# Loading v in four-token runs, w_in in halves, and a written-out order for the first seventeen attention slots

## Chip, cores and metric

One core of a Trainium2 chip runs the whole kernel. The metric is device time in microseconds (us) of one execution. Five engines work side by side, each through its own instructions in the order in which they were written: TensorE (PE in the profile: matmuls, and transposes done as matmuls; PEld is its weight load), VectorE (DVE), ScalarE (ACT), GpSimd (POOL) and SyncE (SP), which here only issues DMAs. GpSimd issues those DMAs that change the type on the way (float32 to bfloat16).

## The reference

Eight batches of eight heads, 576 tokens, head size 64: attention over a sliding window of 128 tokens with a bias that falls linearly with distance, and its output (4,608 rows of 512) through a two-layer network with a hard-swish in between.

```python
scores = scale * np.matmul(q, k.transpose(0, 1, 3, 2))
rel = pos[:, None] - pos[None, :]
bias = slopes[:, None, None] * (-np.abs(rel).astype(np.float32))[None, :, :]
mask = (rel >= 0) & (rel < window)            # window = 128
scores = np.where(mask, scores + bias[None], -1000000000.0)
attn = np.exp(scores - np.max(scores, axis=-1, keepdims=True))
attn = attn / (np.sum(attn, axis=-1, keepdims=True) + 1e-09)
attn_out = np.matmul(attn, v)
# x = attn_out as [4608, 512]
h = x @ w_in                                   # w_in [512, 2048]
g = h * np.clip(h + 3.0, 0.0, 6.0) / 6.0
out = g @ w_out                                # w_out [2048, 512]
```

All inputs and the output are float32; the matmuls run in bfloat16.

## The kernel before

**Attention.** Two heads make a pair, so there are 32 pairs ("slots" in the steady part), four to a batch: pairs 0 to 3 are batch 0, pairs 4 to 7 batch 1. For a pair, q and k are wanted with the head size on the partitions. For batch 0 they come as nine-token runs (`load_run`, line 90), are cast by `prepare` (line 204), transposed on TensorE by 18 small matmuls for q and 18 for k (`transposes`, line 211) and copied out of PSUM. For batches 1 and 2, and for half of batch 3, four heads are transposed together, nine full transposes at a time (`prepare_double` line 223, `wide_double` line 248, `double` line 236). The rest goes through `tbuf` and a transposing DMA (`xbar`, line 197). `scores_diag` (line 285) and `scores_off` (line 313) are 8 and 10 matmuls of 64 rows, two heads in turn, for the block on the diagonal and the block beside it; `tables_diag` and `tables_off` (lines 266 and 299) add bias and mask by matmuls for the first pairs. ScalarE takes the exponential, GpSimd masks where no table did. `attend` (line 406) or `values` (line 394) multiply by v with a column of ones and divide by the sum. `back` (line 421) turns the result so that the model dimension lies on the partitions (the ring `xT`): by five transposes on TensorE and a copy for pairs 0 to 7, 10 and 11, by a transposing DMA issued by SP for the others.

**v.** `load_tokens` (line 108) brings v with one token on each partition, which makes the pieces 256 bytes long. `cast_v` (line 179) or `cast_tokens` (line 183) cast it into `vbuf`.

**The network.** Tokens go in nine groups of 512. A unit "up" (`moe_up`, line 462) is four matmuls of 512 columns, ScalarE's part of the activation and VectorE's; sixteen of them fill `gbuf`. A unit "down" (`moe_down`, line 488) is four matmuls of 512 columns; four of them make 128 rows of the output. `load_w_in` brings a quarter of w_in (line 165), `load_w_out` a quarter of w_out (line 170), both on GpSimd's queue. The probabilities of batch 0 are kept in the room of `w_out_sb`, those of batch 1 in `gbuf[1]` (`rooms`, line 274).

**Order.** Nothing is reordered by a compiler: every engine works in the order of the code. `first_batch` (line 558) does the four pairs of batch 0 whole, then `second_batch` (line 618) works batch 1 with up units between, and `segment` (line 669) works slots 8 to 31, each slot with seven or eight units put in by `fill` (line 523), which takes them from the list `units`. After the last slot only units are left.

## Time and profile before

| | |
|---|---|
| median of three runs | 323.52 us (323.32 to 324.7) |
| the profiled execution, its own time | 323.3 us |
| its span, first to last instruction | 321.6 us |
| granted TensorE clock, mean | 0.998 |
| first matmul of an up unit | at 22.0 us |
| first matmul of a down unit | at 51.71 us |
| first matmul of the last rows of the output | at 314.98 us |

The span is divided in the page into 40 slices of some 8 us. A digit is the busy share of an engine in tenths, 9 being 90% or more. "Busy" of a matmul runs to its modelled end, and matmuls overlap, so a stretch can count as busy although the next matmul starts late; the distances between starts in the timeline show that. A row of the timeline names the start, the length, the engine, the line of the kernel, what is written from what, and how many alike were merged; an idle time before it stands in brackets with what ended it.

### The profile page before, as it was taken

The page shows a single profiled execution, that of the slowest core. Times are in us where ns is not written, and L with a number is a line of the kernel's source. Part 1 is how long each engine was busy: PE and PEld are TensorE (multiplying, and loading weights), DVE is VectorE, ACT ScalarE, POOL GpSimd, SP SyncE. Part 2 cuts the span into 40 slices and gives each one's busy share as a digit, 9 for nine tenths or more (in the row PEclk, how much of TensorE's full clock was granted, in tenths as well). Part 3 has the DMA queues.
Part 4 walks back from the last instruction along what each step waited for, and adds up shares of the span by engine and source line. Part 5 has one row for each costly group of instructions (what it writes and reads, how often), then busy time and mean ns, then how long its engine had stood idle before and what let it go on. Part 6 is the DMA issues. An engine that isn't in the chain of part 4 may idle for free.

```text
span 321.6 us, 7050 instructions
## 1 busy us (share of the span) xinstructions
PE 312.4 (97%) x2738; PEld 167.6 (52%) x2738; DVE 173.0 (54%) x338; ACT 195.6 (61%) x334; POOL 141.1 (44%) x249
## 2 busy tenths in 40 slices
PE   7889999999999999999999999999999999999996
PEld 5565465455555554554667654554554444444443
DVE  6667674554456555555555555555655455455510
ACT  3758976877767766766676667666764344244401
POOL 8455493594493767366745665463331000000000
PEclk9999999999999999999999999999999999999999
DMA  7999999899999999999999989922112200000112
GB/s 276 202 333 208 247 270 196 210 258 194 212 248 166 244 201 203 193 229 199 192 199 202 237 173 212 214 72 86 23 53 66 75 34 35 33 33 33 67 53 77
DMA packets 131425, 51.90 MB, mean 161 GB/s; under 512 B 118976, under 2 KB 123328, under 8 KB 131392
## 3 DMA queue, kind: packets, MB, share of 16 engines
q1 hardware_dynamic: 126160, 45.36, 66.2%
q0 software_dynamic: 4224, 4.19, 8.2%
q10 hardware_dynamic: 1008, 1.90, 1.6%
q8 instruction: 21, 0.34, 0.5%
q14 instruction: 12, 0.10, 0.1%
HBM read 36.70 MB, written 9.44 MB: 143 GB/s over the span
## 4 chain that ended last, share of the span: by engine, by line
PE 82%; DMA 10%; SPq 2%; POOL 2%; DVE 1%; ACT 1%; issue 1%; POOLq 0%
PE ops L501 37%; PE hps L451 33%; DMA w_out_sb<-in_moe_w_out_dram 5%; DMA ldbuf<-in_v_dram 3%; PE scd L296 3%; DMA ldbuf<-in_k_dram 2%; PE av L391 2%; SPq L112 2%; PE av L383 2%; PE sco L328 1%; PE ops L482 1%; PE w L153 1%; POOL w_out_sb L171 1%; PE tp L219 0%; ACT kTb L244 0%
## 5 line engine op out<-in xcount | busy, mean ns | idle before, releaser
L471 DVE SCALAR_TENSOR_TENSOR gbuf<-r,hps 128x512 bf16<-128x512 f32 x144 | 98.7, 687 | 102.5 <-ACT r L470 100.2
L470 ACT ACTIVATE r<-hps,bias 128x512 f32<-128x512 f32 x144 | 98.9, 689 | 88.9 <-PE hps L451 88.7
L451 PE MATMUL hps<-xT,w_in_sb 128*128 128x512 bf16 (+1 forms) x640 | 144.8, 358 | 0.5 <-ACT xT L438 0.3
L501 PE MATMUL ops<-w_out_sb,gbuf 128*128 128x512 bf16 x560 | 137.8, 379 | 0.3 <-DMA w_out_sb<-in_moe_w_out_dram 0.3
L451 PEld LDWEIGHTS <-w_in_sb 128*128 128x128 bf16 x640 | 59.2, 98 | 54.8 <-issue 0.8
L501 PEld LDWEIGHTS <-gbuf 128*128 128x128 bf16 x560 | 51.8, 98 | 56.7 <-issue 0.6
L354 POOL TENSOR_SCALAR_AFFINE_SELECT pd<-pd 128x512 bf16<-128x512 bf16 x48 | 29.7, 634 | 34.5 <-ACT pd L351 34.5
L364 POOL TENSOR_SCALAR_AFFINE_SELECT po<-po 128x512 bf16<-128x512 bf16 x48 | 30.3, 636 | 32.5 <-ACT po L361 32.3
L351 ACT ACTIVATE pd<-scd,bias_d 128x512 bf16<-128x512 f32 x48 | 31.7, 685 | 4.7 <-PE scd L296 4.7
L510 DVE COPY osb<-ops 128x512 f32<-128x512 f32 x33 | 22.7, 687 | 20.4 <-PE ops L501 20.2
L361 ACT ACTIVATE po<-sco,bias_o 128x512 bf16<-128x512 f32 x48 | 33.0, 688 | 0.0
L194 POOL CAST tbuf<-ldbuf 128x512 bf16<-128x512 f32 (+1 forms) x45 | 25.6, 614 | 16.7 <-DMA qTb<-tbuf 9.0
L402 DVE TENSOR_TENSOR avs<-av,rc 128x384 bf16<-128x384 f32 (+1 forms) x48 | 23.6, 491 | 1.6
L391 PEld LDWEIGHTS <-pd 128*128 128x128 bf16 x192 | 14.3, 97 | 8.3 <-issue 0.5
L383 PE MATMUL av<-vbuf,po 128*128 128x65 bf16 x192 | 18.0, 193 | 0.0
L391 PE MATMUL av<-vbuf,pd 128*128 128x65 bf16 x192 | 17.3, 194 | 0.3 <-ACT kTb L244 0.3
L187 POOL CAST vbuf<-ldbuf 128x1024 bf16<-128x1024 f32 x14 | 14.3, 1044 | 4.3 <-DMA ldbuf<-in_v_dram 4.3
L383 PEld LDWEIGHTS <-po 128*128 128x128 bf16 x192 | 14.3, 98 | 2.9 <-DVE avs L402 0.5
L367 ACT ACTIVATE p4buf<-sco,bias_d 128x64 bf16<-128x64 f32 x48 | 15.5, 324 | 0.0
L227 POOL CAST pr<-ldbuf 128x576 bf16<-128x576 f32 x20 | 12.9, 670 | 5.0 <-DMA ldbuf<-in_k_dram 3.1
L296 PE MATMUL scd<-qTb,kTb 64*128 64x128 bf16 x256 | 12.7, 219 | 1.7 <-DVE kTb L220 0.9
L296 PEld LDWEIGHTS <-kTb 64*128 64x128 bf16 x256 | 7.2, 94 | 13.4 <-issue 9.7
(96 smaller groups left out, 217.4 us busy)
## 6 DMA issues: line engine op xcount, KB each, us to landing
out_dram<-osb SPq DMA_DIRECT2D x33, 256.0 KB, 2.4
ldbuf<-in_v_dram SPq DMA_DIRECT2D x32, 256.0 KB, 5.6
ldbuf<-in_q_dram SPq DMA_DIRECT2D x20, 256.0 KB, 4.9
ldbuf<-in_k_dram SPq DMA_DIRECT2D x16, 256.0 KB, 4.5
ldbuf<-in_q_dram SPq DMA_DIRECT2D x12, 288.0 KB, 7.3
ldbuf<-in_k_dram SPq DMA_DIRECT2D x12, 288.0 KB, 7.6
w_in_sb<-in_moe_w_in_dram POOLq DMA_DIRECT2D x4, 512.0 KB, 8.8
w_out_sb<-in_moe_w_out_dram POOLq DMA_DIRECT2D x4, 512.0 KB, 11.6
```

The source lines that it names most:

```text
L194: nc.gpsimd.tensor_copy(out=tbuf[:m, :, j, :], in_=s[:m, j, :, :].rearrange("p (i e) d -> p i (e d)", e=2))
L296: nc.tensor.matmul(scd[:, e, ts(j, 128)], lhsT=kT[r, j, :], rhs=qT[r, j, :], start=first, stop=first or j == 3)
L351: nc.scalar.activation(out=pd[:, e, :, :].rearrange("p j c -> p (j c)"), in_=sc[:, e, :], func=ACT.Exp, bias=bias_d[:, h:h + 1], scale=scale)
L354: nc.gpsimd.affine_select(out=pd[:, e, :, :], in_=pd[:, e, :, :], pattern=[[0, 4], [1, 128]], channel_multiplier=-1, base=0, compare_op=AL ...
L361: nc.scalar.activation(out=po[:, e, :, :].rearrange("p j c -> p (j c)"), in_=sc[:, e, :], func=ACT.Exp, bias=bias_o[:, h:h + 1], scale=scale)
L364: nc.gpsimd.affine_select(out=po[:, e, :, :], in_=po[:, e, :, :], pattern=[[0, 4], [-1, 128]], channel_multiplier=1, base=-1, compare_op=A ...
L383: nc.tensor.matmul(out_av, lhsT=po[:, e, qt % 4, :], rhs=vb[:, qt - 1, h, :], start=True, stop=False)
L391: nc.tensor.matmul(out_av, lhsT=d, rhs=vb[:, qt, h, :], start=(qt == 0), stop=True)
L451: nc.tensor.matmul(hps[:, lo:hi], lhsT=w_in_sb[:, ks, ts(ms, 128)], rhs=xT[:, ks, ds(src, hi - lo)], start=(ks == 0), stop=(ks == n_ks - 1))
L470: nc.scalar.activation(out=r6, in_=hps, func=ACT.Relu, bias=bias3[:, 0:1], scale=1.0 / 6.0)
L471: nc.vector.scalar_tensor_tensor(out=gts[nt][:, ms, :], in0=r6, scalar=1.0, in1=hps, op0=ALU.min, op1=ALU.mult)
L501: nc.tensor.matmul(ops[nt, sub], lhsT=gts[nt][:, ms, ts(sub, 128)], rhs=w_out_sb[:, ms, :], start=(ms == 0), stop=(ms == n_ms - 1))
```

## The change

Seven parts, all of them in the part of the kernel before slot 20.

- v of batches 0 and 1 is loaded with four consecutive tokens on a partition (`s_ldv`), two DMAs of four heads each for tokens 0 to 511, in pieces of 1,024 bytes; the last 64 tokens still come token by token (`s_ldl`, cast by `s_cl`). Two casts (`s_cr`) put it into `vruns`, which lies in `tbuf`. Matmuls with a selection matrix put the tokens back in order: `s_vp` makes two groups of 128 tokens, eight matmuls of 32 rows and 512 columns, in two row groups by turns, and `s_ve` copies each group of 128 tokens from PSUM into `vbuf`. The selection matrix `sel` is made on VectorE at the start by one memset and 16 small copies.
- w_in is loaded by two DMAs of half its columns (`s_wp`) in place of four of a quarter (`load_w_in`).
- The results of pairs 4, 5 and 6 go to `xT` by a transposing DMA (`s_bx`); pair 7 still goes by TensorE.
- The products with v of batch 0 are cut differently: `s_vf` makes the first three groups of 128 tokens of a pair, `s_vr` one group of several pairs at once, `s_vl` four groups of pair 3. The backs of batch 0 are four groups a pair, and one matmul group for the last 64 tokens of all four pairs (`s_br`).
- `warm_up` issues 27 matmuls in place of 30; `p4buf` has four buffers in place of two.
- `first_batch`, `second_batch` and the slots up to 19 are replaced by `PLAN`, a text with one step a line, which `run_plan` issues in order; an argument V, P or A names the engine of a copy. Each engine gets its own steps out of it in the order of the lines. `segment` starts at slot 20. The order of up and down units between (`ORDER`) is fitted to it.
- In the plan the loads and the masks of slots 8 to 16 stand in another order, too: loads of the next batches are spread piece by piece among the other steps.

The steps named below: `c0` casts and `t0` transposes q or k of a pair of batch 0, `e0` copies the result; `td`, `to`, `sd`, `so` are the tables and scores; `xt`, `xd`, `xo` exponentials; `pd`, `dt`, `de` cast, transpose and copy four heads of a later batch; `vf`, `vr`, `vl` multiply by v, `nf`, `nr`, `nl` divide; `bf` transposes back and `ef` copies to `xT`; `u` is the four matmuls of an up unit, `ur` and `um` its activation. After the part of the plan that is printed come the other fifteen up units of the first group of tokens, the second batch with `vp 1 0 h o` and `vp 1 2 h av`, the four `wout`, which stand between the up units, `bx 5`, `bx 4`, `bx 6`, `bk 7`, and then `d 0 0 0 h`, the first down unit, behind five up units of the second group.

```diff
+    sel = perm.tile([128, 4 * 130], BF16)
...
-    def second_w_in():
-        nc.gpsimd.memset(w_out_sb[:, 4, 0:1], 0.0)
-        load_w_in(1)
...
-    ORDER = [("UUDUDUUDUD", "UUDUDUDUD", "UDUDUDD", "UUDDDD"),
+    ORDER = [("UUDUDUUDUDUUDUDUDUDUDUDUDDUUDDDD",),
...
-    def first_batch():
-        prepare(0, (V, A))
...
-    def second_batch():
-        for g in range(NP, 2 * NP - 1):
...
+    def s_c0(g, nm, eng):
+        pr = prs.tile([128, RT * D], BF16, tag=f"pr{nm}", name="pr",
+                      padded_shape=[128, 2 * RT * D])
+        C[eng](out=pr, in_=runs[nm][:, g % NP, :])
+        st[g, nm] = pr
...
+    def quads(tag, n):
+        if tag == "sc":
+            return psum(tag, 1024).rearrange("p (g c) -> p g c", c=256)[:, 0:n, 0:2 * W].rearrange(
+                "p g (e c) -> p g e c", e=2)
+        return psum(tag, n * 2 * W).rearrange("p (g e c) -> p g e c", g=n, e=2)
...
+    def s_vf(g, tag):
+        av = st["vf", g] = quads(tag, 3)
+        av_matmuls(g, range(3), lambda qt, e: av[:, qt, e, :])
...
+    def s_vr(g0, n, qt, tag):
+        av = st["vr", g0, qt] = quads(tag, n)
+        for i in range(n):
+            av_matmuls(g0 + i, (qt,), lambda _, e: av[:, i, e, :])
...
+    def s_ub(nt, ms, n, tag):
+        hps = psum(tag, 512)
+        up_mms(nt, ms, 0, n, hps)
+        st["u", nt, ms] = hps, n
...
+    def s_u(nt, ms, tag):
+        hps, n = st.get(("u", nt, ms), (None, 0))
+        if hps is None:
+            hps = psum(tag, 512)
+        up_mms(nt, ms, n, n_ks, hps)
+        st["u", nt, ms] = hps, n_ks
+        at[0] += 1
...
+    SEL = sel[:, 0:4 * 129].rearrange("p (t c) -> p t c", t=4)
+    vruns = tbuf.rearrange("p h j c -> p (h j c)")[:, 0:4 * H * D].rearrange(
+        "p (t h d) -> p t h d", t=4, h=H)
+
+    def s_sel():
+        nc.vector.memset(sel, 0.0)
+        diag = sel.rearrange("p (t c) -> p t c", t=4)[:, :, 0:128:4]
+        for j in range(4):
+            r = slice(32 * j, 32 * j + 32)
+            for t in range(4):
+                nc.vector.tensor_copy(out=diag[r, t, :], in_=ident[r, r])
...
+    def s_ldv(b, h, n):
+        nc.sync.dma_start(out=vsource(b)[0][:, ds(h, n), :],
+                          in_=v[b, ds(h, n), 0:512, :].rearrange("h (p t) d -> p h (t d)", t=4))
...
+    def s_cr(b, h, n, eng):
+        C[eng](out=vruns[:, :, ds(h, n), :].rearrange("p t h d -> p h t d"),
+               in_=vsource(b)[0][:, ds(h, n), :].rearrange("p h (t d) -> p h t d", t=4))
+
+    def unshuffle(b, h, n, j0, banks):
+        for t in range(4):
+            for i, ps in enumerate(banks):
+                r = slice(32 * (j0 + i), 32 * (j0 + i) + 32)
+                nc.tensor.matmul(ps, lhsT=SEL[r, t, 0:128], rhs=vruns[r, t, ds(h, n), :],
+                                 start=(t == 0), stop=(t == 3))
...
+    def s_vp(b, j0, t1, t2):
+        banks = [psum(t, 512).rearrange("p (h d) -> p h d", h=H) for t in (t1, t2)]
+        for i in range(2):
+            st["vu", b, 0, j0 + i] = banks[i].rearrange("p (j h) d -> p j h d", j=1)
+        unshuffle(b, 0, H, j0, banks)
+
+    def s_ve(b, h, n, j0, nj, eng):
+        C[eng](out=vbuf[b % 2][:, ds(j0, nj), ds(h, n), 0:D], in_=st["vu", b, h, j0])
+
+    def s_wp(i, k0, n):
+        nc.gpsimd.dma_start(out=w_in_sb[:, ds(k0, n), ts(i, 1024)],
+                            in_=moe_w_in[ds(k0 * 128, n * 128), ts(i, 1024)].rearrange(
+                                "(k p) f -> p k f", p=128))
...
+    def s_bx(g):
+        b, hp = divmod(g, NP)
+        nc.sync.dma_start_transpose(
+            out=xT[:, hp, ds(b % 4 * S, SP)].rearrange("p (j c) -> p j c", j=NQ),
+            in_=st[g, "avs"].rearrange("p j e d -> p (j e d)"))
...
+    def run_plan(text):
+        for line in text.split("\n"):
+            if line.strip():
+                name, *args = line.split()
+                STEPS[name](*(int(a) if a.isdigit() else a for a in args))
...
+    PLAN = """
+sel
+wu 20
+td 0
+wu 7
+c0 0 k A
+c0 0 q A
+mem 3
+t0 0 k o
+e0 0 k V
+ldv 0 4 4
+c0 1 q A
+c0 2 k P
+t0 0 q h
+e0 0 q A
+ldv 0 0 4
+t0 1 q o
+c0 1 k A
+sd 0
+xt 0
+to 0
+t0 1 k h
+e0 1 k A
+c0 2 q P
+t0 2 k h
+ldd 1 0 q 1
+c0 3 q V
+ldl 0
+e0 1 q V
+cr 0 4 4 V
+cr 0 0 4 P
+td 1
+e0 2 k A
+so 0
+t0 3 q h
+ldd 1 0 q 0
+xo 0
+c0 3 k V
+ldd 1 1 k 1
+sd 1
+t0 2 q o
+xt 1
+to 1
+ldd 1 0 k 0
+so 1
+td 2
+e0 2 q V
+sd 2
+xo 1
+ldd 1 0 k 1
+t0 3 k h
+e0 3 k V
+to 2
+xt 2
+e0 3 q V
+vp 0 2 o av
+so 2
+xo 2
+vp 0 0 h h
+ve 0 0 8 3 1 V
+ve 0 0 8 0 1 A
+ve 0 0 8 2 1 V
+ve 0 0 8 1 1 V
+vf 0 av
+td 3
+pd 1 0 k 0 V
+pd 1 0 k 1 V
+to 3
+vr 0 3 3 o
+ldd 1 1 k 0
+wp 0 0 4
+vf 2 h
+mem 2
+pd 1 0 q 0 P
+nr 0 3 3
+nf 2
+sd 3
+so 3
+xt 3
+pd 1 0 q 1 P
+vf 1 o
+nf 1
+xo 3
+nf 0
+dt 1 0 q 0 9 sc
+cl 0 P
+bf 1 h
+ef 1 0 512 A
+mem 4
+de 1 0 q 0 9 V
+bf 0 h
+vl 3
+pd 1 1 k 0 P
+bf 2 h
+pd 1 1 k 1 P
+vr 2 2 4 av
+nl 3
+dt 1 0 k 0 9 sc
+ldv 1 4 4
+de 1 0 k 0 9 V
+cr 1 4 4 P
+nr 2 2 4
+ef 0 0 512 A
+bf 3 o
+to 5
+ldd 1 1 q 0
+ef 3 0 256 A
+vr 0 2 4 h
+wp 1 0 4
+ef 2 0 512 A
+ldd 1 1 q 1
+sd 5
+ef 3 256 256 A
+xd 5 1
+pd 1 1 q 0 V
+so 5
+u 0 5 h
...
             load_run(g, "q", nc.sync)
-        load_tokens(0, "v")
         constants()
         memsets()
-        memsets_later()
-        first_batch()
-        second_batch()
-        fill(2)
-        segment(2 * NP, G, lambda g: FILLS.get(g, (1, 1, 1, 2, 0, 1, 2)))
+        run_plan(PLAN)
+        done[0] = 20 - 1
+        segment(20, G, lambda g: FILLS.get(g, (1, 1, 1, 2, 0, 1, 2)))
         done[0] = G
         fill(len(units))
 
```

## The prediction

> **What bounds the kernel now.** I read the page's engine shares first, then the sums by stage, then TensorE's timeline of the stages that are not full, then the DMAs that these stages wait for.

> ```profile
> span 321.6 us, 7050 instructions
> PE 312.4 (97%) x2738; PEld 167.6 (52%) x2738; DVE 173.0 (54%) x338; ACT 195.6 (61%) x334; POOL 141.1 (44%) x249
> ...
> PE   7889999999999999999999999999999999999996
> ```

> ```profile
> 0.00:8.00 8.00, 5.83 (x74) 4.64 (x76) 4.80 (x31) 2.80 (x4) 6.49 (x21) 1.00 0.78 275
> 8.00:16.00 8.00, 6.96 (x178) 4.28 (x180) 4.92 (x9) 6.00 (x6) 3.36 (x5) 1.00 1.09 204
> 16.00:24.00 8.00, 6.64 (x127) 5.39 (x128) 5.44 (x12) 4.37 (x7) 4.76 (x8) 1.00 1.10 333
> 24.00:52.00 28.00, 27.50 (x315) 15.74 (x313) 18.97 (x30) 24.42 (x37) 18.73 (x29) 1.00 1.14 235
> 52.00:96.00 44.00, 43.03 (x374) 22.24 (x373) 22.39 (x43) 31.71 (x58) 27.30 (x46) 1.00 1.08 222
> 96.00:240.00 144.00, 144.00 (x1280) 78.49 (x1279) 80.83 (x161) 97.30 (x181) 78.97 (x139) 1.00 0.92 174
> ```

> After the stretch come busy times of TensorE, its weight load, VectorE, ScalarE, GpSimd, then clock, DMA share and GB/s. From 96 us TensorE is full, and ScalarE, the next, has 97.30 of 144 us. So the change can win only before 96 us, and every matmul that it adds costs its full time unless it falls into a wait. The idle sum before 96 us is 6.0 us (96 less 89.97), and the timeline shows waits that the sum hides:

> ```profile
> 43.71 0.59 PE L451 MATMUL hps<-xT,w_in_sb 128*128 128x512 bf16 x2
> 44.44 0.45 PE L432 MATMUL tb<-ident,avs 128*128 128x128 bf16 x5
> ...
> 46.14 0.44 PE L432 MATMUL tb<-ident,avs 128*128 128x128 bf16 x5
> 46.73 0.45 PE L242 MATMUL tp<-ident,pr 128*128 128x128 bf16 x5
> ...
> 47.61 0.45 PE L432 MATMUL tb<-ident,avs 128*128 128x128 bf16 x5
> 48.27 0.38 PE L242 MATMUL tp<-ident,pr 128*128 128x128 bf16 x4 [0.21 <-ACT kTb L244]
> ...
> 57.70 1.03 PE L451 MATMUL hps<-xT,w_in_sb 128*128 128x512 bf16 x4
> 59.05 1.02 PE L501 MATMUL ops<-w_out_sb,gbuf 128*128 128x512 bf16 x4 [0.33 <-DMA w_out_sb<-in_moe_w_out_dram]
> ```

> Four matmuls of 512 columns take 0.86 us where nothing waits (the chain shows them so throughout), a transpose of 128 columns 0.056. So 57.70 to 59.05 hides 1.35 - 0.86 = 0.49 us of waiting for w_out; the three rows before it hide 0.30, 0.31 and 0.38 us beside the turning back of pairs 4 to 6. In the same way I find 0.30 at 54.8, 0.33 and 0.15 at 71 to 73, 0.14 and 0.34 at 79 to 81, and 0.18, 0.23 and 0.24 from 89 to 92: together 3.4 us of waits between 25 and 96 us.

> **The change, part by part.**

> *The selection matmuls.* The trace has no 32-row matmul. The nearest rows are the scores: 64 rows, two heads in turn, eight of 128 columns from start to next work in 0.33 us, where eight full ones take 0.45; starts lie 3 and 28 ns apart by turns, so two row groups run together. If the 32-row ones do the same, eight of 512 columns take four times 0.216 = 0.87 us, else 1.73. I take 0.87, since the form is the same but for the rows, and keep 1.73 for the range. [...] Here a change to the scores and back costs 0.10 and 0.12 us over the plain distance, so I add 0.2: 1.07 us a `vp`, 4.3 us for four. The two of batch 0 are in the chain below; the two of batch 1 stand among up units, where TensorE is full: **+2.1 us**.

> *Their copies.* Each group of 128 tokens is one PSUM copy of 512 columns, 0.69 us on VectorE by the `osb` row (0.59 on ScalarE). Four a batch replace the five casts of v (0.56 each on VectorE, 0.62 on GpSimd), and the two casts of runs (1.04 us by the 1,024-element GpSimd row) come on top. In batch 1 the up units cover them (VectorE 18.97 of 28 us); without that cover a copy would hold `av` for 0.7 us. The selection matrix is 17 small VectorE operations, some 0.07 each by the bias rows (eight in 0.58): 1.2 us, under ScalarE's casts, which end later.

> *The first 25 us, by hand.* TensorE finishes 27 warm-ups and one set of tables at 5.14 (in place of 30 and two sets at 6.45). The first k cast ends at 5.4 as before, q's now follows on ScalarE; its copy ends at 7.15, so the first scores start at 7.2 (before: 7.94). ScalarE's copies and VectorE's cast of q of pair 3, whose load lands near 9, hold the second scores to 10.15 (10.26). VectorE then takes the first half of v. Runs end near 9 and v passes 4,096 packets of 256 bytes now; half of it as 512 long ones lands near 11, so that cast ends at 12 and the third scores start at 12.95 (13.12). GpSimd's half lands near 12.3 and ends at 13.6. `vp 0 2` runs to 15.1, `vp 0 0` to 16.25. Here is the first new wait: `vf 0` needs all four copies, the last at 17.1: 0.85 us in which `td 3`, `to 3` and pair 3's scores queue behind it, with their exponentials. From there the exponentials of pair 3 (two of 0.95 us) and VectorE's divisions (0.6 each) and copies (1.35) give `dt` at 20.4, `vl` at 21.4, `dt 1 0 k` at 22.25, `sd 5` at 24.35 and the first up unit at 25.0. Before, the first up matmul runs at 22.0, and by 25.0 seven are done (1.5 us), transposes for 0.75 and the row back of 0.22; after, transposes for 1.0 and the tables and scores of pair 5 for 1.2 are done ahead. That is 2.5 against 2.2 us of work, within my rounding: **0.0 us**. So 1.07 us a `vp` and the new wait are paid with the earlier start and fuller slots, not saved.

> *Pairs 4 to 6 by DMA.* Fifteen transposes go: 15 x 0.056 = **-0.84 us**, and 3 ScalarE copies of 0.64 us. The transposing DMAs have 22 rows in the trace, 2.5 us to landing; the tokens are wanted by the second group of up units, more than 4 us later. SP must wait for the divided result, and behind it stand the next loads of q and v; the trace has SP's loads waiting 2 us and more without loss.

> *The reordering.* The 3.4 us of waits belong to the code that is replaced: 1.0 to the turning back (gone), 0.5 to w_out (four loads issued at 41.2 to 43.5, now from some 32 on, since batch 0's probabilities are read by then), the rest to a transpose or product placed behind a copy. Bounds: all of it stays (0) or all goes (-3.4). I take the whole **-3.4**, the up units of the group now standing between nearly every pair of dependent steps, with ScalarE as the tightest cover: 24.42 of 28 us busy before, about the same after.

> *w_in in halves.* See the second rival; in the forecast it costs nothing.

> *Sum.* 2.1 + 0.0 - 0.84 - 3.4 = -2.1 us. On the profiled execution's own 323.3 us (span 321.6 and 1.7 around it; median 323.52) this gives **321.2 us**.

> **The rivals.**

> *Waits only move.* A fixed order has its own places where a copy is late, and the new one has more dependent steps (cast, selection, copy, product). Then 3.4 us stay: 323.3 + 2.1 - 0.84 = 324.6 us. For it: my chain to 25 us still has 4.6 us of waits, as many as before. Against: after 25 us there are up units to put between.

> *w_in arrives late: the slower side.* One half is one DMA with one completion, issued on GpSimd behind `cr 0 0 4 P`, so at about 14 us (before: a quarter at 12.4). All of TensorE's plan behind `u 0 5` waits for it, and then ScalarE and VectorE.

> ```profile
> 44.00:47.00 3.00, 2.71 (x39) 1.77 (x38) 2.93 (x7) 1.89 (x4) 3.00 (x6) 1.00 1.18 187
> ...
> DMA to landing us min/median/max: 6.3/8.8/9.5
> ```

> A quarter took 6.3 to 9.5 us. With weights alone on the queues 187 GB/s land, so the second 0.52 MB adds 2.8 us: 9.1 to 12.3, landing at 23.6 to 26.8. If six loads of k, q and v of batch 1 share as they did at 18.7, the time doubles to 12.6 to 19. It decides from a landing at about 28.7, where the wait of 3.7 us eats the gain and 0.5% more; at 30 us: 321.2 + 5.0 = 326.2. [...]

> *Row groups don't run together.* 16 pairs x 0.216 = 3.5 us more: 324.7 us.

> *The start gains too.* If half of the 4.6 us of waits that my chain has left is my rounding: 321.2 - 2.3 = 318.9 us. v's shorter transfer speaks for it:

> ```profile
> 9.00:12.00 3.00, 2.69 (x70) 1.72 (x70) 1.56 (x3) 2.44 (x3) 1.07 (x3) 1.00 1.36 226
> 19.50:22.50 3.00, 2.65 (x53) 2.28 (x52) 2.73 (x5) 1.58 (x3) 1.41 (x3) 1.00 1.04 406
> ```

> The upper stretch carries v's 256-byte pieces, the lower q and k in pieces of 2,304: 226 against 406 GB/s. v's 1.05 MB go from 4.6 us to between 2.6 and 4.6.

> **How the numbers follow.** Forecast 0.36, start gains too 0.20, waits only move 0.17, w_in late 0.20, row groups 0.07. A measurement of this kernel tells 0.5% (1.6 us: under 321.9, over 325.1) from no change. Faster: 0.31 of the forecast, the 0.20 of the start and 0.03 of the others, 0.54. Slower: 0.17 of w_in's and 0.05 of the two others, 0.22. The rest, 0.24, is the same. The range goes from 318.9 to 325.8, which leaves out w_in's later landings. The forecast's own is 319.9 to 322.6, by a third of the 3.4 us either way.

> **What would show it.** Eight 32-row matmuls in 0.9 us; the first up matmul near 25 us with no wait for w_in; a w_out wait gone; no row of turning back for pairs 4 to 6; TensorE's starts without gaps over 0.15 us from 25 to 96 us. A gap of microseconds before `u 0 5` would make the forecast wrong, as would up units that wait for ScalarE's banks.

## The result, and the profile after

| | before | after |
|---|---|---|
| median of four runs | 323.82 us (323.32 to 324.7) | 333.46 us (331.35 to 336.76) |
| ratio, 95% interval | 1 | 1.0273 (1.0217 to 1.0328): slower |
| the profiled execution, its own time | 323.3 us | 336.76 us |
| its span | 321.6 us | 335.0 us |
| first matmul of an up unit | at 22.0 us | at 29.23 us |

The profiled execution of after is the longest of the four, 3.3 us above their median, and lies so far above the fastest that the ratio, one of means, leaves it out; what it shows is the change and some 3 us of spread, which the experiments come back to. The head of its page and two of the rows in 40 slices:

```profile
span 335.0 us, 7024 instructions
PE 315.2 (94%) x2713; PEld 170.6 (51%) x2752; DVE 184.5 (55%) x372; ACT 196.9 (59%) x339; POOL 131.8 (39%) x236
...
PE   7987899699999969999999999999999999999995
...
PEclk9999999899999997999999999999999999999999
```

The row of before was a row of nines from the fourth slice on. Here slices 3, 7 and 14 (counted from 0, of 8.4 us each: 25 to 33, 59 to 67 and 117 to 126 us) stand out, and in slices 7 and 15 the granted clock falls (8 and 7 tenths). One caution: 2,713 matmul records stand beside 2,752 weight loads, so 39 matmul records are missing and the busy sum of TensorE is too low. The waits, which have a row of their own, are the safer reading. The waits of TensorE in after, with the releaser, the sum, how many, and the longest:

```profile
PE bank L791 <- DMA w_out_sb<-in_moe_w_out_dram: 3.0, 1, 3.0
PE scd L278 <- DMA kTb<-tbuf: 2.5, 1, 2.5
PE bank L433 <- DMA w_in_sb<-in_moe_w_in_dram: 2.1, 1, 2.1
PE w L156 <- POOL ident masks.py:199: 1.4, 1, 1.4
PE bank L756 <- POOL pr L747: 1.0, 1, 1.0
```

Only the fourth is as in before. The other four are new (for w_out, before waited 0.33 us), each is a single stall, and three of them end with a DMA. TensorE's timeline at the three longest:

```profile
26.79 0.36 PE L310 MATMUL sco<-qTb,kTb 64*128 64x128 bf16 x8
29.23 1.90 PE L433 MATMUL bank<-xT,w_in_sb 128*128 128x512 bf16 x7 [2.07 <-DMA w_in_sb<-in_moe_w_in_dram]
...
61.15 1.03 PE L791 MATMUL bank<-w_out_sb,gbuf 128*128 128x512 bf16 x4
65.22 3.52 PE L791 MATMUL bank<-w_out_sb,gbuf 128*128 128x512 bf16 x8 [3.04 <-DMA w_out_sb<-in_moe_w_out_dram]
...
125.68 0.40 PE L278 MATMUL scd<-qTb,kTb 64*128 64x128 bf16 x8 [2.52 <-DMA kTb<-tbuf]
126.54 4.22 PE L433 MATMUL bank<-xT,w_in_sb 128*128 128x512 bf16 x11
```

The second cost of a stall is in the lengths behind it. Eight matmuls of 512 columns take 1.89 us where the clock is full (at 71.17 us); the eight behind the w_out wait take 3.52, the eleven behind the k wait 4.22, where eleven at full clock took 2.54 in one of the experiments (at 122.98 us, the selection matmuls twice). TensorE came back at half its clock (0.50 from 65.15 to 68.56 and from 126.59 to 130.00 us), some 1.6 us lost each time.

Why did the DMAs land so late? Two were queued behind a wait of the engine that issues them. GpSimd's timeline:

```profile
14.12 1.04 POOL L866 CAST tbuf<-ldbuf 128x1024 bf16<-128x1024 f32 x1 [4.66 <-DMA ldbuf<-in_v_dram]
15.11 0.88 POOL L892 DMA_DIRECT2D w_in_sb<-in_moe_w_in_dram  x1
...
37.26 0.66 POOL L747 CAST pr<-ldbuf 128x576 bf16<-128x576 f32 x1 [5.42 <-DMA ldbuf<-in_q_dram]
...
40.63 0.67 POOL L747 CAST pr<-ldbuf 128x576 bf16<-128x576 f32 x1
...
45.48 0.77 POOL L174 DMA_DIRECT2D w_out_sb<-in_moe_w_out_dram  x1
53.86 0.63 POOL L636 TENSOR_SCALAR_AFFINE_SELECT pd<-pd 128x512 bf16<-128x512 bf16 x1 [7.61 <-ACT pd L630]
54.45 0.77 POOL L174 DMA_DIRECT2D w_out_sb<-in_moe_w_out_dram  x1
```

w_in's first half stands behind `cr 0 0 4 P`, which waits 4.66 us for v; it is issued at 15.11 and lands 14.1 us later. The last quarter of w_out (`wout 1`) stands behind `md 8 1`, the mask of slot 8, which waits 7.61 us for ScalarE's exponential; it goes out at 54.45, 9 us behind the quarter ahead of it, and lands at 65.2. The third, k of batch 4 for slot 16, went the same way on SP: `ldt 4 k 2` is issued at 113.92 behind the transposing DMA of q, its cast starts at 117.93, the transposing DMA of k at 119.69, and this lands at 125.6. The shorter stall, on `pr`, has a cast behind it: GpSimd's cast of q of batch 2 waits 5.42 us for its load, which SP had issued at 24.47, and the cast of k that TensorE's transposes want at 41.36 stands behind it, at 40.63.

The sum of what is new: w_in 2.1, the cast of k of batch 2 (`pr` L747) 1.0, w_out 3.0, k of batch 4 2.5, half clock 1.6 and 1.7, together 11.9 us; selection matmuls 4 x 1.03 = 4.1 less 0.84 for the transposes that left. That is 15.2 against the 13.4 us by which the spans differ, and the sum has nothing yet for the rest of the start. So old waits did go: by the distances between TensorE's starts from 31 to 96 us, only gaps of 0.2 to 0.3 us at 35.6, 50.9 and 51.5 us are left beside these stalls, where the kernel before had 3.4 us of them.

### The profile page after: what moved, and what is told of

Its sections match the earlier page's. It is cut to its first block, busy times and chain, and to the rows that moved or that the text cites. A ratio compares the mean times of both kernels' runs of the same rounds, so it can differ in the third digit from the quotient of the medians.

```text
span 335.0 us, 7024 instructions
## 1 busy us (share of the span) xinstructions
PE 315.2 (94%) x2713; PEld 170.6 (51%) x2752; DVE 184.5 (55%) x372; ACT 196.9 (59%) x339; POOL 131.8 (39%) x236
## 4 chain that ended last, share of the span: by engine, by line
PE 77%; DMA 17%; ACT 2%; DVE 1%; issue 1%; POOL 1%; SPq 0%; DVEq 0%; POOLq 0%
PE ops L483 24%; PE hps L433 21%; PE bank L433 11%; PE bank L791 11%; DMA w_in_sb<-in_moe_w_in_dram 4%; DMA w_out_sb<-in_moe_w_out_dram 3%; DMA ldbuf<-in_v_dram 3%; DMA xT<-avs 2%; DMA ldbuf<-in_k_dram 2%; PE av L373 2%; PE scd L278 2%; DMA kTb<-tbuf 2%; PE av L365 2%; PE sco L310 1%; PE ops L464 1%
## 5 line engine op out<-in xcount | busy, mean ns | idle before, releaser
L452 ACT ACTIVATE r<-hps,bias 128x512 f32<-128x512 f32 x83 | 57.1, 689 | 65.9 <-PE hps L433 64.9
L453 DVE SCALAR_TENSOR_TENSOR gbuf<-r,hps 128x512 bf16<-128x512 f32 x83 | 57.1, 688 | 59.9 <-ACT r L452 59.0
L483 PE MATMUL ops<-w_out_sb,gbuf 128*128 128x512 bf16 x354 | 87.5, 379 | 1.5 <-issue 1.0
L433 PE MATMUL hps<-xT,w_in_sb 128*128 128x512 bf16 (+1 forms) x390 | 82.5, 344 | 0.2
L433 PE MATMUL bank<-xT,w_in_sb 128*128 128x512 bf16 x231 | 60.5, 388 | 3.0 <-DMA w_in_sb<-in_moe_w_in_dram 2.1
L779 ACT ACTIVATE r<-bank,bias 128x512 f32<-128x512 f32 x61 | 41.8, 693 | 30.9 <-PE bank L433 28.9
L784 DVE SCALAR_TENSOR_TENSOR gbuf<-r,bank 128x512 bf16<-128x512 f32 x61 | 41.4, 686 | 33.6 <-ACT r L779 33.2
L791 PE MATMUL bank<-w_out_sb,gbuf 128*128 128x512 bf16 x175 | 45.1, 390 | 3.6 <-DMA w_out_sb<-in_moe_w_out_dram 3.0
L346 POOL TENSOR_SCALAR_AFFINE_SELECT po<-po 128x512 bf16<-128x512 bf16 x24 | 15.2, 636 | 20.2 <-ACT po L343 20.2
L636 POOL TENSOR_SCALAR_AFFINE_SELECT pd<-pd 128x512 bf16<-128x512 bf16 x24 | 14.9, 634 | 14.1 <-ACT pd L630 9.6
L904 POOL TENSOR_SCALAR_AFFINE_SELECT po<-po 128x512 bf16<-128x512 bf16 x24 | 15.1, 634 | 13.5 <-ACT po L898 11.0
L937 POOL CAST tbuf<-ldbuf 128x512 bf16<-128x512 f32 (+1 forms) x25 | 14.6, 612 | 14.5 <-DMA ldbuf<-in_q_dram 8.0
L898 ACT ACTIVATE po<-sco,bias_o 128x512 bf16<-128x512 f32 x24 | 16.4, 693 | 1.6 <-PE sco L310 1.6
```

The source lines that it names most:

```text
L433: nc.tensor.matmul(hps[:, lo:hi], lhsT=w_in_sb[:, ks, ts(ms, 128)], rhs=xT[:, ks, ds(src, hi - lo)], start=(ks == 0), stop=(ks == n_ks - 1))
L452: nc.scalar.activation(out=r6, in_=hps, func=ACT.Relu, bias=bias3[:, 0:1], scale=1.0 / 6.0)
L453: nc.vector.scalar_tensor_tensor(out=gts[nt][:, ms, :], in0=r6, scalar=1.0, in1=hps, op0=ALU.min, op1=ALU.mult)
L483: nc.tensor.matmul(ops[nt, sub], lhsT=gts[nt][:, ms, ts(sub, 128)], rhs=w_out_sb[:, ms, :], start=(ms == 0), stop=(ms == n_ms - 1))
L779: nc.scalar.activation(out=r6, in_=st["u", nt, ms][0], func=ACT.Relu, bias=bias3[:, 0:1], scale=1.0 / 6.0)
L784: nc.vector.scalar_tensor_tensor(out=gts[nt][:, ms, :], in0=st["r", nt, ms], scalar=1.0, in1=st["u", nt, ms][0], op0=ALU.min, op1=ALU.mult)
```

## The experiments

Five groups of kernels ran, each group on one chip beside the kernel before, whose medians there were 323.2 to 324.2 us. Versions of the kernel after spread by 0.3 to 7.6 us between four executions, the kernel before by 1.3 to 2.5 between seven or six, so a single microsecond between two groups is not resolved.

### The stalls, taken one by one

**A quarter of w_out asked for earlier** (in after).

```diff
 wout 0
+wout 1
...
-wout 1
```

> The changed kernel with one step moved: the load of the second quarter of w_out is issued right behind the first quarter's, instead of behind the first mask of slot 8. Theory of queued loads: the 3.2 us wait at 61.8 us goes, and with it the 1.7 us in which eight matmuls run at half clock after it: 333.5 - 4.9 = about 328.6 us. Rival, that the waits only move on to the next late load: less than 2 us are gained, 331.5 us or more.

Measured: 329.65 us (328.15 to 331.29), ratio 1.0213 (1.017 to 1.0257), 3.8 us less than after by the medians; the intervals of the two ratios overlap, so it is the rows that show the gain. The wait on w_out is gone from the trace, and so is the half clock there. That is as expected by the theory: 3.0 of wait and 1.6 of clock, less what moved (a wait of 1.4 us for the columns of `xT` at 52 us is new).

**Dummy matmuls in that wait** (in after), to separate the wait from the clock.

```diff
+warm 14 av
 d 0 0 1 h
```

> The changed kernel with 14 matmuls of 512 columns (3.0 us) whose result is not used, ahead of the down unit that waits 3.2 us for w_out. If the half clock after that wait comes from TensorE's standing still, these fill the wait, the eight slow matmuls run at 0.216 us in place of 0.427, and 1.7 us are gained: 331.8 us. Rival, that the clock falls for another reason: no gain, or 3 us lost if the wait isn't there.

Measured: 331.73 us (329.28 to 331.94), 1.7 less than after by the medians, which is inside the spread. TensorE's timeline where the wait was:

```profile
57.98 3.18 PE L605 MATMUL bank<-tab,ident 128*128 128x512 bf16 x14 [0.25 <-DVE gbuf L784]
61.00 1.89 PE L791 MATMUL bank<-w_out_sb,gbuf 128*128 128x512 bf16 x8
```

The late quarter of w_out was issued at 50.25 us here, and the slowest of the four took 10.1 us to land; if it was this one, TensorE would have waited to 60.4. Fourteen matmuls whose result is not used fill that time, and the eight behind them take 1.89 us instead of 3.52. So of the 4.6 us lost at this place in after a third was the clock and not the wait. (The profiled execution, 329.28 us, is the fastest of the four; it had no wait on w_in either.)

**One k load earlier**: the third group of tokens of batch 4 asked for right behind the second (with the w_out quarter early).

```diff
 ldt 4 k 1
+ldt 4 k 2
...
-ldt 4 k 2
```

> The kernel with the early w_out load, and one load of k of batch 4 issued with the others, ahead of a transposing DMA that holds SP's queue until 113 us. The casts of k for slot 16 then don't wait for it, the transposing DMA of k is issued some 1.5 us earlier, and the 2.1 to 2.7 us wait at slot 16 becomes about 1 us, with the half clock after it gone: 329.65 - 1.5 to -3.5, so 326 to 328 us. Rival, that this transposing DMA must wait for the one of q anyway: less than 0.7 us.

Measured: 327.99 us (327.17 to 328.97), ratio 1.0142 (1.0109 to 1.0175); 1.7 less than without, on another chip. The wait on `kTb` fell from 2.1 to 1.6 us only: the next link, GpSimd's casts behind the transposing DMA of q, was nearly as late. It is the fastest version of all, and still 4.2 us behind the kernel before on its chip. Its trace still has the selection matmuls (4.1 us) and waits of 1.6 us for k and 1.3 us for the columns of `xT`; how the 4.2 us divide was not measured.

**w_in in four quarters again** (with the w_out quarter early).

```diff
-wp 0 0 4
+win 1
+win 0
...
-wp 1 0 4
+win 2
+win 3
```

> The last kernel with the early w_out load, and w_in in four quarters at the places of the two halves, the quarter of the first up unit first. If the size of the half is what makes w_in late, the first up unit no longer waits and the second, which needs the other quarter, waits for the rest: up to 0.9 us gained in executions where the wait is there (2.3 us in the profile of the changed kernel, none in that with the early w_out load): 328.5 to 329.7 us against 329.65. Rival, that the second DMA only adds its own start: no gain or a loss of up to 1 us.

Measured: 329.07 us (328.96 to 329.27), ratio 1.0175 (1.0148 to 1.0202), 0.6 less than the version with halves. No wait on w_in in its trace; but the profiled execution with halves had none either, so the difference is not shown to come from there. What it does show is the spread: 0.3 us between four executions.

**One quarter ahead of the cast of v** (as the last, `win 1` ahead of `cr 0 0 4 P`).

> As the kernel with quarters, but the first quarter is issued ahead of GpSimd's half of the v cast, near 9.5 us in place of 13 to 15, while GpSimd stands idle for v. If the issue behind that cast is what makes w_in late, no up unit waits and the later loads on GpSimd's queue come earlier too: 327 to 328.5 us. Rival, that the DMA engines are full from 9 to 27 us and the early quarter pushes v, k and q of batch 1 back by up to 3 us: 330 us or more.

Measured: 331.0 us (329.85 to 333.67), 1.9 more. The queue order did hold w_in back, but pulling it forward took the DMA engines from k of batch 1: its loads go out at 12.0 us in both versions, and VectorE's cast of it starts at 20.70 us in place of 17.73, so TensorE waits 2.3 us for VectorE's divisions at 21 us. The rival holds: the DMA share was 1.04 and 1.13 in the two stretches of 5 us from 5 to 15 us. (The profiled execution, the slowest of the four, also ran at half clock from 7.9 to 11.3 us, so its rows do not give the size.)

**The selection matrix later** (in the 327.99 us version, `sel` moved to just ahead of `cr 0 4 4 V`).

> The kernel after with the fourth quarter of w_out asked for right behind the third, batch 4's k load of three tokens early (the version of 327.99 us), and the building of the selection matrix moved on VectorE from the front to just ahead of the first unshuffled cast of v. The theory that the sixteen copies of 1.87 us at 4.79 stand ahead of the first key eviction and push the whole start back expects TensorE's wait on `kTb` L625 (1.3 us) to go or to fall below 0.5, the first scores at 7.4 or before instead of 8.1, and 326.7 to 327.2 (0.8 to 1.3 less). The rival, that the start is set by the casts and loads behind (v, then w_in), expects the start's gain to be waited away before the first up matmul: 327.7 to 328.3, with a wait on v or w_in that is longer by as much.

Measured: 333.4 us (331.67 to 336.15). The first scores did start at 7.41, as expected, and then this came; VectorE's row and TensorE's:

```profile
10.57 2.74 DVE L846 COPY sel<-ident 32x32 bf16<-32x32 bf16 x16
...
15.42 0.40 PE L278 MATMUL scd<-qTb,kTb 64*128 64x128 bf16 x8 [2.88 <-DVE qTb L625]
```

The sixteen small copies cost 1.87 us of VectorE at the front and 2.74 at 10.57. At the front, where VectorE otherwise waits for the first transposes, they cost 0.5 (k's first copy starts at 6.68 with them ahead, at 6.15 without); at 10.6 they stood ahead of a cast and a copy that TensorE wanted. Half clock followed, at 0.50 from 17.1 to 23.9 and from 27.4 to 30.8 us, and is part of the 5.4 us. Both theories of the expectation were too kind to the move.

### Parts of the change alone, in the kernel before

**w_in in two halves.**

```diff
-            out=w_in_sb[:, :, ts(g, 512)],
+            out=w_in_sb[:, :, ts(g, 1024)],
```

> The kernel before with w_in in two halves, nothing else: the first is issued where the first quarter was, the second where the third was. If a half is late because of its size, the first up matmul waits past 22.0 us: issued at 12.4, landing after 11 to 14 us, 23.4 to 26.4 us, so 1.4 to 4.4 us more on TensorE: 325 to 328 us. Rival, that the size is harmless and in the changed kernel only the later issue (15.1 us) counts: 323.8 us, no change.

Measured: 326.85 us (326.35 to 327.28), ratio 1.0109 (1.0078 to 1.014): 3.4 us more, for this part alone. The longest wait of TensorE:

```profile
PE hps L450 <- DMA w_in_sb<-in_moe_w_in_dram: 3.0, 1, 3.0
```

The halves, issued at 12.3 and 29.2 us, landed 12.5 and 9.7 us later; a quarter had taken 6.3 to 9.5. The first up matmul waits for the whole half, 3.0 us, to 24.84, and from 26.2 to 29.6 us TensorE runs at half clock.

**Pairs 4, 5 and 6 back by transposing DMA.**

```diff
-        if by_xbar(g):
+        if by_xbar(g) or g in (4, 5, 6):
```

> The kernel before with the results of pairs 4, 5 and 6 turned by transposing DMAs on SP, nothing else. If these DMAs are good by themselves, fifteen transposes (0.84 us) and some 1.0 us of waits between 43 and 49 us go: 322 us. If SP, which waits for each divided result with its loads queued behind, is what makes loads late, the loads of batch 2 and 3 slip by some us and the time rises, 325 us or more.

Measured: 348.77 us (348.19 to 350.41), ratio 1.0796 (1.0755 to 1.0837): 25 us more: the rival's side (325 or more), but not by its mechanism, since here the loads stand ahead of the DMAs and not behind them. SP's timeline and one row of VectorE:

```profile
48.34 11.02 SPq L112 DMA_DIRECT2D ldbuf<-in_v_dram  x5
...
59.41 2.57 SPq L98 DMA_DIRECT2D ldbuf<-in_k_dram  x4
62.03 6.42 SPq L112 DMA_DIRECT2D ldbuf<-in_q_dram  x5
68.55 5.80 SPq L425 DMA_TRANSPOSE xT<-avs  x3
72.30 0.82 DVE L413 TENSOR_TENSOR avs<-wide,rcw 128x640 bf16<-128x640 f32 x1 [25.03 <-DMA xT<-avs]
```

Fourteen loads stand on SP ahead of the three transposing DMAs and hold it for 20 us. `avs` has two buffers, so VectorE stops at the third pair for 25.03 us, and TensorE behind it for 24.4 in one wait. The DMA itself is quick (2.5 us to landing, the median of 22 in the trace of before); its place in a queue and the buffer that it holds are the price. This part can only be had together with a new order of the loads.

### v in runs of four tokens

**v of both batches by tokens in the kernel after**, no selection matmuls.

```diff
-ldv 0 4 4
-vp 0 2 o av
-ve 0 0 8 3 1 V
+ldt 0 v 0
+cv 0 3 V
```

(and so on for each load, cast and group of both batches)

> The changed kernel with v of batches 0 and 1 loaded token by token and cast as before; the selection matmuls are left out, all else stays. Theory of queued loads: four times 1.03 us of selection matmuls and the 1.0 us wait for their copies go, while v lands later by 2 us or so; the waits for w_in, w_out and k stay: 329 to 331 us. Rival, that the selection is the main loss: 325 us or less.

Measured: 336.96 us (334.3 to 340.95), ratio 1.0395 (1.0317 to 1.0474), 3.5 slower than after. Its longest wait, on the casts of v at the start:

```profile
PE bank L373 <- DVE vbuf L180: 4.7, 1, 4.7
```

Both theories were wrong: in this plan, which was written for them, the runs of four tokens pay for their matmuls. (The intervals of the two ratios just touch, and the profiled execution, the longest of the four, also has 17 us at half clock; the wait in the row is what shows the reason.)

**The selection matmuls of batch 1 twice** (in the 327.99 us version).

```diff
+        for _ in range(1 + b):
-        unshuffle(b, 0, H, j0, banks)
+            unshuffle(b, 0, H, j0, banks)
```

> The version of 327.99 us with the 16 selection matmuls of batch 1 run twice into the same two banks, so the result is the same and only TensorE's work is doubled. The prediction's term (1.07 us a pair of row groups, all of it on TensorE's path) expects 2.1 us more: 329.8 to 330.4. The rival, that they lie in time in which TensorE waits anyway, expects 327.9 to 328.5.

Measured: 330.61 us (329.52 to 334.53), 2.6 more on another chip: the theory's side, though with this spread the time alone would not settle it. The rows do. First the version with one pass, two calls of `s_vp`; then the doubled one:

```profile
33.11 1.03 PE L873 MATMUL bank<-tbuf,sel 32*128 32x512 bf16 x8
34.68 1.04 PE L873 MATMUL bank<-tbuf,sel 32*128 32x512 bf16 x8 [0.21 <-DVE gbuf L784]
```

```profile
32.18 1.90 PE L873 MATMUL bank<-tbuf,sel 32*128 32x512 bf16 x16
34.34 1.90 PE L873 MATMUL bank<-tbuf,sel 32*128 32x512 bf16 x16
```

Eight more matmuls add 0.87 us, four times 0.216: the two row groups do run together.

### Steps moved, and buffers

**Two waits given other work** (in the 327.99 us version).

```diff
-ub 1 0 3 av
-bk 7 o
-ek 7 V
...
 u 0 13 h
+ub 1 0 3 av
+bk 7 o
+ek 7 V
...
-sd 16
...
 u 2 11 o
+sd 16
```

> The version of 327.99 us with two steps moved on TensorE: the run of up units of batch 1 that reads the pairs brought back by transposing DMA (and what comes behind it for pair 7) behind up unit 13 of batch 0, and the scores of slot 16 behind up unit 11 of batch 2, each so that matmuls which wait for nothing run during the wait. The theory that the written-out order alone makes these two waits (1.3 us on xT and 1.6 us on kTb) expects both to fall below 0.4 us and 325.0 to 325.8. The rival, that what they wait for is behind its consumers whatever is put between, expects the slots behind to stall in turn (probabilities of slot 16 late, value matmuls waiting): 327.0 to 328.5.

Measured: 331.22 us (330.85 to 334.69), 3.2 more: the rival's side, and beyond it. The two waits, 1.3 and 1.6 us, came back as 3.5 and 1.9 us a step later. VectorE and TensorE at the first place:

```profile
53.44 0.82 DVE L731 TENSOR_TENSOR avs<-wide,rcw 128x640 bf16<-128x640 f32 x1 [2.72 <-DMA xT<-avs]
54.19 1.27 DVE L784 SCALAR_TENSOR_TENSOR gbuf<-r,bank 128x512 bf16<-128x512 f32 x2
54.92 3.15 PE L433 MATMUL bank<-xT,w_in_sb 128*128 128x512 bf16 x7 [3.45 <-DVE gbuf L784]
```

The up unit that was put into the gap needs a bank. The eviction that frees it (L784) stands on VectorE behind the division of pair 7, and that waits for an `avs` buffer which a transposing DMA still reads. The seven matmuls of the last row ran at half clock (0.50 from 53.5 to 60.3 us).

**Two more `avs` buffers, nothing moved.**

```diff
-        avs = st[g, "avs"] = small.tile([128, NQ, 2, D], BF16, tag="avs", name="avs")
+        avs = st[g, "avs"] = small.tile([128, NQ, 2, D], BF16, tag=f"avs{g}" if g in (5, 7) else "avs",
+                                   name="avs", bufs=1 if g in (5, 7) else 2)
```

> The version of 327.99 us with buffers of their own for `avs` of pairs 5 and 7, nothing else moved. The theory that VectorE stands at pair 7's normalization for an `avs` buffer which a transposing DMA still reads (2.1 us at 51.4, with the evictions that free TensorE's banks queued behind it) expects no wait on xT<-avs over 0.3 us at TensorE or VectorE between 45 and 60 us, and 326.3 to 327.2. The rival, that TensorE waits for the columns of xT themselves and the buffer is a bystander, expects VectorE's wait to go and TensorE's 1.3 us to stay, and 327.7 to 328.3.

Measured: 331.23 us (328.15 to 335.74). VectorE's wait is gone and TensorE's on `xT` is 1.8 us: the rival holds for the wait, the columns themselves are late. The time is no use here, since this profiled execution waited 2.5 us for w_in, which its parent's did not.

**Buffers and the first move together.**

> The buffers for pairs 5 and 7, and the run of up units of batch 1 moved on TensorE behind up unit 13 of batch 0 (the first of the two moves tried before). The theory that the move failed because VectorE stood for an `avs` buffer with the evictions behind it expects TensorE's wait near 52 us below 0.5 us (1.8 with the buffers alone, 3.5 with the move alone). The rival, that up unit 13 waits for a bank whose eviction is late in any case, expects a wait on gbuf L784 or xT of 1.3 us or more. The time, whose runs spread by 3 us and more for these versions, is expected at 327 to 331 and decides nothing.

Measured: 329.49 us (327.94 to 332.53). At the place TensorE waits 0.9 and 0.5 us, where it was 3.5 with the move alone and 1.8 with the buffers alone. That is between the two expectations: the buffer did defeat the move, but up unit 13 then meets the next late eviction.

**Buffers and quarters of w_in.**

> The buffers of the first run of these and w_in in four quarters in the order 1, 0, 2, 3, which gave 0.6 us less once. If the two add: 0.4 to 0.8 less than the first of these, 325.7 to 326.6. If the quarters only helped where w_in decided: the same within 0.3.

Measured: 330.7 us (327.39 to 331.98), 0.5 less than the buffers alone, inside the spread. Not decided.

**Pairs 4 to 6 by matmuls again** (in the 327.99 us version).

```diff
-bx 5
+bk 5 o
+ek 5 V
```

(and the same for 4 and 6)

> The version of 327.99 us with pairs 4, 5, 6 brought back by TensorE and VectorE as in the kernel before, five transposes and one eviction of 0.46 us each, in the places where the transposing DMAs were issued. The prediction's term (0.84 us of TensorE saved by the DMAs at no other cost) expects 328.8. The theory that the DMAs hold SP for 8.8 us at 40.6 with the loads of batch 3 behind, and two buffers, expects the wait at 52 us to go and 326.0 to 327.5; a late engine, VectorE with three more evictions, would keep it at 328 or more.

Measured: 331.76 us (330.53 to 333.03), beside 331.23 for the buffers on the same chip. The wait at 52 us is gone and one of 0.9 us for a bank is there. Its profiled execution waited 2.0 us for w_in. So in the new order the DMAs do cost a wait on `xT` (1.3 us in the version that this one starts from), and the matmuls bring another, shorter one. In time nothing is resolved: the version is 3.8 us slower than its parent, but on another chip and with that wait for w_in. The predicted saving of 0.84 us is neither shown nor refuted.

**Everything together**: both moves, the later `sel`, w_in in quarters.

> Both of the two before together, and w_in in four quarters again in the order 1, 0, 2, 3. The theory that the change's own parts cost little beside the waits of its written-out order (and that their costs add) expects 323.6 to 324.8, that is the time before within 0.4%. The rival, that the transposing DMAs and the selection matmuls cost more than their place shows, expects 325.5 or more with no single wait over 1 us in the trace behind 25 us.

Measured: 336.19 us (332.06 to 336.69): worse than after. The waits that the single moves made are all in it, 5.0 us on evictions (L784) and 1.7 on q's copy, and behind them TensorE ran at half clock from 15.5 to 25.7 and from 59.8 to 63.2 us.

**The same, with v of batch 1 by tokens.**

> The kernel of the run before, with v of batch 1 alone by tokens: no four-token runs, no selection matmuls and no mode changes for batch 1, five token loads instead. The theory that batch 1's selection costs its 16 matmuls on TensorE (2.1 us by the pitch of 1.03 us a pair of row groups) expects 2.0 us less than the run before, 321.5 to 322.8, and with that faster than the kernel before. The rival, that the token loads hold the DMA engines and SP for longer just where w_in and k, q of batch 2 are wanted, expects the same or up to 3 us more, with a wait on vbuf, w_in or on q of batch 2 in the trace between 27 and 50 us.

Measured: 339.25 us (337.85 to 341.01), 3.1 more again: the rival. TensorE has a wait in it that the run before has not, and SP's timeline says why:

```profile
PE wide L756 <- DVE pr L747: 2.7, 1, 2.7
```

```profile
16.26 7.38 SPq L657 DMA_DIRECT2D ldbuf<-in_v_dram  x3
23.75 4.08 SPq L650 DMA_DIRECT2D ldbuf<-in_q_dram  x2
```

Three token loads of v hold SP for 7.38 us, the q loads of batch 1 stand behind them, and VectorE's cast of that q (L747) comes late.

## Why the prediction was wrong

**The step that failed is the reordering, taken whole at -3.4 us.** The old waits did nearly all go, as the starts from 31 to 96 us show. What failed are the bounds, "all of it stays (0) or all goes (-3.4)": they treat an order as something that only takes waits away, because there is work to put between. The runs showed that the new order makes waits of its own, 8.6 us of stalls in the profile and 3.3 us of half clock behind them, and that the longest are not made by TensorE's neighbours but by DMAs that are issued late, each behind a waiting instruction on GpSimd or SP: 9 us for a quarter of w_out behind a mask, 4.66 us for w_in behind a cast. The loads of w_out, said to go out "from some 32 on", went out at 39.0 to 54.45 us. The prediction followed TensorE's chain by hand to 25 us and no queue after that; had it walked GpSimd's steps between the four `wout`, the mask of slot 8 ahead of the last was there to be read. It also had no term for time lost behind 96 us, although the plan rewrites the slots up to 19: the stall for k of slot 16 and its half clock, 4.2 us, lie at 125 us. Asking for that quarter earlier gave back 3.8 us by the medians, the k load 1.7 more.

**"w_in in halves: in the forecast it costs nothing"** was wrong by 2.1 us in the profile (issue at 15.11, where about 14 was said, landing after 13.6 to 14.1, where 9.1 to 12.3 was said), and by 3.4 us in the kernel before. The rival had the mechanism, and the half did land at 29.2, past the 28.7 from which it was said to decide; but its own arithmetic gives 325.4 us for that landing, and none of the rivals reaches 333. In six other profiles with halves the first was issued at 13.1 to 13.3 us, a half took 10.9 to 13.5 us, and TensorE, not ready before 26.6, did not wait for it. Over all the runs with halves the measured landings are 9.7 (the kernel before with halves) to 14.3 us (the buffers alone). Other loads ran beside them: in after the DMA share was 1.05 from 9 to 27 us.

**Half clock after a stall** was in no term: 1.6 and 1.7 us in the profile, and with the dummy matmuls the eight slow ones took 1.6 us less. It is not the whole loss: of the four executions of after, the one that ran at a granted clock of 1.000 took 331.35 us, still 7.5 more than the kernel before.

**The first 25 us at 0.0** were off by 2 us: the first up unit was ready at 27.16 (29.23 less the wait of 2.07), not 25.0, and in the six other profiles it ran at 26.6 to 28.2. The sixteen copies of the selection matrix took 1.87 us, 2.2 with their memset, where 1.2 was said, and not hidden under ScalarE's casts but ahead of VectorE's first copy of k (which starts at 6.68). The first scores came at 8.12 and not 7.2, 0.5 us of it by these copies. The rest is slower matmuls: in this execution TensorE ran slowly up to about 11 us, 36 transposes in 1.11 us at 9.62 where before has 0.76 at 6.45, the eight first scores in 0.61 where the second take 0.40, and the second scores came at 11.94, where the version with the w_out quarter early has them at 10.72. v's second half landed at 14.1, but at 12.1 to 12.3 in the six other profiles, where 12.3 was said. The wait of `vf 0` was foreseen at 0.85 and came with 0.67.

**Pairs 4 to 6 by DMA at -0.84** rested on "SP's loads waiting 2 us and more without loss". In after, SP stands from 26.3 to 41.6 us for the first divided result, with the next loads behind it; the loads of q and k of batch 2 had gone out before, at 19.2 to 25.8, and no wait of TensorE in after is shown to come from this. In the kernel before, the same DMAs behind the loads cost 25 us. In the new order the cost is the wait on `xT`, 1.1 to 1.8 us, in the versions where w_out is no longer late.

**Right** were the selection matmuls (0.97 us from the start of a `vp` to the next work and 0.10 more than the plain distance ahead of it, 0.15 us from the last matmul of 128 columns at 15.28 where 0.056 is plain, for 1.07; the row groups run together) and that runs of four tokens shorten the start by more than they add: without them the plan is 3.5 us slower. Two slips touch no term: the starts of the scores lie 3 and 53 ns apart by turns, not 3 and 28, and a third of the 3.4 us either way makes the forecast's own range 320.1 to 322.3 us, not 319.9 to 322.6.

## What to carry to other kernels

Before a new written-out order is believed, walk each engine that issues DMAs, instruction by instruction, and ask of every transfer what waiting instruction stands ahead of it and who stops when it lands late; an order that is full on TensorE says nothing about that. A stall of TensorE may have a half-clock stretch behind it, which cost 1.6 to 1.7 us here and followed each of the twelve stretches of the clock's grid in which TensorE stood still for more than 2.06 us (next section). A transfer that lands close to its use can make the time differ from execution to execution: here TensorE waited 2.0 to 2.5 us for w_in in three profiles and not at all in six (next section). To put work into a gap, check first that its bank and its eviction are free of what makes the gap.

## What the runs showed of the hardware

**Whether the clock fell depended on where the stall lay, not on its length alone.** The same wait for k of slot 16 in two kernels, first with the quarter of w_out early, then with pairs 4 to 6 by matmuls:

```profile
118.77 0.40 PE L278 MATMUL scd<-qTb,kTb 64*128 64x128 bf16 x8 [2.14 <-DMA kTb<-tbuf]
119.42 2.75 PE L433 MATMUL bank<-xT,w_in_sb 128*128 128x512 bf16 x12
```

```profile
121.68 0.40 PE L278 MATMUL scd<-qTb,kTb 64*128 64x128 bf16 x8 [2.14 <-DMA kTb<-tbuf]
122.54 4.22 PE L433 MATMUL bank<-xT,w_in_sb 128*128 128x512 bf16 x11
```

2.14 us of wait in both; twelve matmuls at full clock in the one, eleven at half in the other. At this place waits of 2.52, 2.51, 2.40, 2.35, 2.29 and 2.14 us were followed by half clock, waits of 2.38, 2.27, 2.14 and 2.12 were not. The granted clock in the traces shows what sets them apart. Behind the two waits in after half clock lasted 3.41 us; in the other traces it lasted 3.4 us too (26.2 to 29.6 us with w_in in halves in the kernel before), or two or three times that (17.1 to 23.9 us with the selection matrix later, 15.5 to 25.7 with everything together). Within each of these executions its stretches start on one grid of 3.41 us (in after at 65.15 and 126.59 us, 18 times 3.413 apart; with everything together at 15.5 and 59.8, 13 times), and the grid lies elsewhere in each: worked out from these starts, its first line in the span is at 0.30 us in after, at 1.89 and 3.31 us in the two kernels of the rows above. Two neighbouring stretches of that grid in each of the two kernels (length and busy time of TensorE first, its clock third from the end):

```profile
114.53:117.94 3.41, 2.10 (x17) 0.89 (x15) 2.44 (x6) 1.95 (x3) 1.87 (x3) 1.00 1.01 197
117.94:121.36 3.42, 2.59 (x28) 1.43 (x28) 0.29 (x2) 1.39 (x3) 0.61 (x1) 1.00 1.09 281
```

```profile
119.36:122.77 3.41, 1.22 (x21) 0.75 (x22) 1.62 (x3) 1.28 (x2) 1.45 (x3) 1.00 0.95 246
122.77:126.19 3.42, 3.42 (x10) 1.18 (x9) 1.35 (x3) 1.44 (x4) 0.61 (x1) 0.50 1.11 240
```

**Two landings of the same load.** In the profiled executions with the same steps up to w_in, GpSimd waits for v either 2.96 to 3.12 us or 4.48 to 4.66 us. In the first case w_in is issued at 13.1 to 13.3, its halves take 11.3 to 12.3 us (medians), and TensorE does not wait for it (six kernels); in the second it is issued at 14.8 to 15.1, the halves take 13.7 to 13.9 us, and TensorE waits 2.0 to 2.5 us (after, the buffers alone, and pairs 4 to 6 by matmuls). With one half-clock stretch (1.6 to 1.7 us) these waits come, as an estimate, to some 4 us between executions of one kernel; why v lands at two times stays open.
